# Tail scores of the experts as 64x64 fp32 products of four heads, short tiles scored in one visit, and a new order of the third stage

## The chip, the cores and the metric

The kernel runs on 1 core of one Trainium2 chip. What counts is the device time of one execution, in microseconds (us). "Before" is the median of 3 runs. One execution of it was taken by the profiler, and every row below is of that one.

## What is computed

Three layers follow one another: windowed attention, a gated feed-forward layer with a mixing matrix over the positions, and four experts of causal attention of which each token takes two. The change lies in the third.

```python
# B, S, D, E, Hd = 4, 576, 512, 4, 64
logits = x @ w_gate
topk = np.argpartition(-logits, 2, axis=-1)[..., :2]      # two experts per token, weights w
for e in range(E):
    q = x @ wq[e]
    k = x @ wk[e]
    v = x @ wv[e]
    scores = scale * (q @ k.transpose(0, 2, 1))
    scores = np.where(causal, -1000000000.0, scores)
    scores = scores - scores.max(-1, keepdims=True)
    a = np.exp(scores)
    a /= a.sum(-1, keepdims=True) + 1e-09
    ye = a @ v @ wo[e]
    # out += w * ye where the token chose e
```

## The kernel before

The program has three stages, one behind the other on every engine: attention and the feed-forward layer with their weights (`OPENING`, `FIRST`, `SECOND`), the fold of two weight matrices into `W` (L902, ends near 268 us), and the experts. In the third stage an expert is called a head; two heads make a pair (`pr` is the pair, `o` the head in it), and the two heads of a pair lie in the two halves of the 128 partitions.

A value that must keep fp32 accuracy is held as two f32r tiles, a high part and a low part, and a product is made in three passes (`PASSES`): high by high, high by low, low by high.

Each of the 4 batches has 576 tokens: four tiles of 128 queries (`j` 0 to 3) and a tail of 64 (`j` 4). The columns of q and k are stored with the 64 of the tail first. The third stage consists of these steps, named as in the table `THIRD`:

- `Q` (`project`, L1001): q or k of a pair, half of the columns, one of three passes, 4 products. `qh` and `ql` copy the high part (ScalarE) and subtract for the low part (VectorE).
- `V` and `vr`: values of a tile and the gate's logits; `g` and `h`: the gate.
- `Z` and `sp` (`spread`, L1015): GpSimd zeroes tiles `qt` of 128 columns per pair and copies the tail's q of each head onto its own 64 columns of its own half of the rows. A product with `qt` over all 128 rows then gives both heads of a pair at once, with zeros in the other quarters.
- `S` (`scores_b`): the scores of a tile, one pair of heads per visit. For `j` < 4 it makes products of 64 rows (L1083), two heads at a time. For the tail it makes products of 128 rows with `qt` (L1088): three stretches of 256, 256 and 64 keys by three passes, nine per visit. Scores stand in PSUM tiles `psB`, of which there are two; the two pairs of tile 0 or 1 share one.
- `l`, `e`, `f`, `m`: least value with the mask (VectorE, L1104, L1108), exponential (ScalarE), factors, scaling (GpSimd, L298). `T`, `w`, `R`: transposition in blocks, by way of DRAM. For the last tiles of batch 3 the transposition is made by TensorE (`t`, `c`).
- `A` (`attend_b`, L1192, fp32): attention; `oh`, `ol` copy it as high and low part into `o` tiles, of which there are `OBUFS`.
- `O`, `oc`, `o` (`out_tile`, L1210): the last projection, copy and store.
- `L`, `GH`, `GL`, `BH`, `BL`: the input of a batch is loaded, and its high and low parts are made. The tiles `x` (batches 0 and 2) and `x2` (batches 1 and 3) are used again, so the parts of batch 3 come after batch 1 has been projected. From batch 2 on, GpSimd makes the low part (L263).

`THIRD` lists the steps in one row, and this row is the order in which each engine gets its instructions: nothing is scheduled afterwards. An engine takes its instructions strictly in that order and waits where an input is not there.

The first stage has products of the form that the change brings, at L525 to L533, 64 rows by 64 columns, fp32, heads in the four quarters of the array. A product of fp32 operands stands in the trace as two records.

Of the kernel before, what the change touches and what calls it, by code (L numbers as in the profile page):

```python
# [119 lines left out]
class Dense:  # L120
# [68 lines left out]
    ql0.1.1.0 Q0.0.0.1.0 g0.0.1 g0.0.0 Q0.0.1.1.0 g0.0.5 g0.0.2 g0.0.6 Q0.0.0.1.1 g0.0.3 g0.0.7 Q0.0.1.1.1 g0.0.4 Q1.1.1.1.0 g0.0.8 Q0.0.0.1.2 g0.0.9
    Q0.0.1.1.2 g0.0.10 qh0.0.0.1 Q1.0.0.1.2 g0.0.11 qh0.0.1.1 ql0.0.0.1 GH2.0 Q1.1.1.1.1 g0.0.12 ql0.0.1.1 Q1.1.1.1.2 qh1.0.0.1 g0.0.13 GL2.0 S0.0.0  # L190
    ql1.0.0.1 qh1.1.1.1 L2.2 S0.1.0 GH2.1 l0.0.0 S0.0.1 l0.0.1 l0.1.0 S0.1.1 e0.0.0 l0.0.2 GL2.1 e0.0.1 V1.4.0 l0.0.3 l0.1.1 e0.0.2 V1.4.1 l0.1.2
    e0.0.3 l0.1.3 Q1.1.0.0.0 e0.1.0 ql1.1.1.1 S0.2.0 e0.1.1 f0.0 e0.1.2 Q1.1.0.0.1 l0.2.0 m0.0.0 e0.1.3 l0.2.1 V1.4.2 m0.0.1 e0.2.0 m0.0.2 Q1.1.1.0.0
# [1133 lines left out]
```

## Time and profile before

| | |
|---|---|
| median of 3 runs | 435.45 us (435.08 to 436.15) |
| the profiled execution | 435.67 us |
| its span, first to last instruction | 433.6 us |
| TensorE's granted clock, mean | 0.999 |
| the third stage | from 268 us to the end |
| last product ends | 429.65 us |

The span of the profile is 2.1 us shorter than the time of the same execution. A view by stretches gives the busy time of each engine in each part of the span. The chain of waits goes back from the last instruction to what released it, and lists the pieces in order of time. A group of equal instructions has a mean length, and matrix products overlap with each other: how much of the line a product takes is read from start to next start, not from its length.

### The profile page before, as it was taken

How to read it: one execution, taken by the hardware profiler on the slowest of the kernel's cores; microseconds unless marked ns; L12 is line 12 of the kernel's file. 1: busy time of each engine (PE TensorE's matmuls, PEld its weight loads, DVE VectorE, ACT ScalarE, POOL GpSimd, SP SyncE). 2: the span in 40 equal slices, each digit the busy share in tenths (PEclk: the TensorE clock that was granted, in tenths of full speed). 3: DMA queues.
4: the chain of work that ended last, by engine and by line, in shares of the span. 5: the costliest groups of instructions: out<-in, count | busy, mean ns of one | idle time of the engine just before them, and what ended most of it. 6: DMA issues, size and time to landing. Idle time of an engine off the chain costs nothing.

```text
span 433.6 us, 11406 instructions
## 1 busy us (share of the span) xinstructions
PE 419.6 (97%) x4055; PEld 376.8 (87%) x4055; DVE 306.9 (71%) x1062; ACT 240.3 (55%) x746; POOL 152.8 (35%) x281
## 2 busy tenths in 40 slices
...
GB/s 246 359 337 255 134 219 181 103 325 237 214 258 117 217 165 114 110 83 55 114 256 255 163 104 0 110 2 69 179 237 281 144 204 220 235 227 250 245 232 122
DMA packets 76940, 80.01 MB, mean 185 GB/s; under 512 B 18002, under 2 KB 52946, under 8 KB 76500
## 3 DMA queue, kind: packets, MB, share of 16 engines
...
q8 instruction: 32, 0.52, 0.5%
q14 instruction: 24, 0.20, 0.2%
...
## 4 chain that ended last, share of the span: by engine, by line
PE 82%; DVE 10%; DMA 3%; ACT 3%; issue 1%; SPq 1%; DVEq 0%; ACTq 0%
PE pq L1001 12%; PE pg L750 11%; PE pu L735 11%; PE pv L672 8%; PE pvB L1025 6%; PE pxB L1192 6%; PE pout_None L1210 6%; PE px L646 5%; PE psB L1083 4%; PE pw L902 4%; DVE p L285 2%; PE psB L1088 2%; PE pg L753 2%; DMA carry<-p 2%; PE ps L529 1%
## 5 line engine op out<-in xcount | busy, mean ns | idle before, releaser
L286 ACT ACTIVATE p<-p,st 128x128 f32<-128x128 f32 x144 | 56.4, 393 | 15.8 <-DVE st L285 11.4
L750 PE MATMUL pg<-wsp,vn 128*128 128x288 f32 x384 | 60.3, 297 | 1.3 <-ACT vn L707 1.0
L750 PEld LDWEIGHTS pg<-wsp,vn 128*128 128x128 f32 x384 | 54.2, 188 | 3.8 <-ACT vn L707 1.2
L735 PE MATMUL pu<-x,win 128*128 128x288 f32 x384 | 57.5, 296 | 0.0
L1001 PE MATMUL pq<-x,W 128*128 128x288 f32 x384 | 57.1, 297 | 0.0
L672 PE MATMUL pv<-win,x 128*128 128x512 f32 x216 | 56.1, 398 | 0.0
L735 PEld LDWEIGHTS pu<-x,win 128*128 128x128 f32 x384 | 53.4, 188 | 1.8 <-issue 0.9
L1001 PEld LDWEIGHTS pq<-x,W 128*128 128x128 f32 x384 | 52.5, 188 | 1.7 <-issue 0.8
L1113 ACT ACTIVATE pB<-pB,stB 128x128 f32<-128x128 f32 (+4 forms) x72 | 41.8, 583 | 13.2 <-DVE stB L1104 4.8
L565 POOL TENSOR_TENSOR p<-p,st 128x512 f32<-128x512 f32 (+1 forms) x28 | 29.9, 1071 | 52.4 <-DVE st L563 16.1
L298 POOL TENSOR_SCALAR pB<-pB,stB 128x384 f32<-128x384 f32 (+4 forms) x64 | 35.7, 576 | 28.9 <-ACT pTB L1182 6.8
L672 PEld LDWEIGHTS pv<-win,x 128*128 128x128 f32 x216 | 38.7, 188 | 8.0 <-issue 1.1
L1104 DVE CUSTOM_DVE_ANT_0 pB<-psB,trit 128x128 f32<-128x128 f32 (+3 forms) x64 | 28.4, 485 | 8.5 <-PE psB L1083 8.4
L285 DVE CUSTOM_DVE_ANT_0 p<-ps,relm 128x128 f32<-128x128 f32 x128 | 30.2, 284 | 1.9 <-DMA carry<-p 1.7
L600 POOL TENSOR_SCALAR_AFFINE_SELECT pU<-pT 128x512 f32<-128x512 f32 (+1 forms) x26 | 16.0, 625 | 40.7 <-DMA pT<-carry 27.8
L1139 DVE STREAM_TRANSPOSE pB<-pB 128x1024 f32<-128x1024 f32 (+3 forms) x28 | 26.7, 977 | 1.6 <-POOL pB L298 1.6
L758 DVE TENSOR_TENSOR g<-u,pg 128x288 f32<-128x288 f32 x32 | 14.3, 448 | 18.5 <-PE pg L753 18.3
L1025 PE MATMUL pvB<-W,x 128*128 128x260 f32 x192 | 27.4, 284 | 0.0
L286 ACT ACTIVATION_READ_ACCUMULATOR p<-p,st 128x1 f32 x144 | 27.2, 189 | 0.0
L1192 PE MATMUL pxB<-pTB,vt 128*64 128x128 f32 (+2 forms) x480 | 26.7, 261 | 0.0
L1192 PEld LDWEIGHTS pxB<-pTB,vt 128*64 128x64 f32 (+1 forms) x480 | 23.2, 136 | 3.7 <-issue 1.3
L1210 PE MATMUL pout_None<-wo,o 128*128 128x512 f32 x102 | 26.4, 400 | 0.0
...
## 6 DMA issues: line engine op xcount, KB each, us to landing
...
```

The costliest lines, as they stand in the source:

```text
L285: lambda: nc.vector.tensor_tensor_reduce(s_view, ps_view, tab, -0.125, FLT_MAX, ALU.add, ALU.min, nm),
L286: lambda: nc.scalar.activation(s_view, s_view, AF.Exp, bias=nm, scale=-1.0, accum_out=sm),
L298: nc.gpsimd.tensor_scalar(p, p, r, 0.0, op0=ALU.mult, op1=ALU.add)
L565: ops["m"] = lambda: nc.gpsimd.tensor_tensor(blocks, blocks, sm.unsqueeze(1).unsqueeze(3).to_broadcast([P, 4, n, 32]), op=ALU.mult)
L672: nc.tensor.matmul(pv, x[i][:, k, t0 : t0 + P], win[j][:, k, 512:1024], start=(n == 0 and k == 0), stop=(n == 2 and k == 3))
L735: nc.tensor.matmul(pu[:, :HALF], win[i][:, k, m * P : (m + 1) * P], x[j][:, k, c], start=(n == 0 and k == 0), stop=(n == 2 and k == 3))
L750: nc.tensor.matmul(pg[:, :HALF], vn[i][k][:, m * P : (m + 1) * P], wsp[j][:, k, c], start=(n == 0 and k == 0), stop=False)
L1001: nc.tensor.matmul(pq[:, :HALF], W[i][c0 // CUT][:, k, c0 % CUT : c0 % CUT + P], G[j][:, k, c], start=(n == k == 0), stop=(n == 2 and k == 3))
L1025: nc.tensor.matmul(pv[:, :260], rows, W[j][1][:, k, 512 - CUT :], start=(n == k == 0), stop=(n == 2 and k == 3))
L1113: nc.scalar.activation(part(i), part(i), AF.Exp, bias=st[:, i : i + 1], scale=-1.0, accum_out=st[:, 4 + i : 5 + i])
L1192: nc.tensor.matmul(px[64 * o : 64 * o + 64, pr, :qn], vt[:kb, c, (2 * pr + o) * 64 : (2 * pr + o) * 64 + 64], rhs(pr, c, o), start=(c == 0 ...
L1210: nc.tensor.matmul(po[:, : c.stop - c.start], o2[i][:, pr, :], wos[j][:, pr, c], start=(n == pr == 0), stop=(n == 2 and pr == 1))
```

## The change

The tail's q and k are no longer spread. `whole` (steps `qf`, `kf`) adds high and low part on GpSimd into fp32 tiles: `q4` (64 columns, both pairs at once) and `k4` (576 columns, one pair at a time, one buffer). `scores_b` for the tail then makes 64x64 fp32 products: the head in the pair decides the half of the rows, the pair decides the half of the output's partitions. So the tail's scores now have the pair on the partitions and the head of the pair in the place where the pair was, and `tail_gate`, `row_min` and `read_back` follow. A visit at index 0 takes 256 keys, at index 1 the other 256 and 64, each for all four heads. For tiles 0 and 1 one visit scores both pairs. `OBUFS` goes from 10 to 8, and `THIRD` is another order. `OPENING`, `FIRST`, `SECOND` and the fold are as they were.

```diff
@@ -33,7 +33,7 @@
 FLT_MAX = 3.0e38
 TOK = [(t * 128, min(128, S - t * 128)) for t in range(5)]
 COL = [64, 192, 320, 448, 0]
-OBUFS = 10
+OBUFS = 8
 CARRIED = 6
 PASSES = ((0, 0), (0, 1), (1, 0))
 ORDER = ((0, 1, 2, 3, 4), (4, 0, 1, 2, 3))
@@ -182,52 +182,51 @@
 THIRD = """
-    L1.0 L1.1 L1.2 L1.3 Q0.1.0.1.0 VZ0 VZ1 Z0 Q0.0.0.0.0 Z1 Q0.0.0.0.1 Q0.1.0.1.1 Q0.1.0.1.2 Q0.0.0.0.2 V0.2.0 qh0.1.0.1 qh0.0.0.0 V0.0.0 ql0.1.0.1
...
+    L1.0 L1.1 L1.2 L1.3 Q0.1.0.1.0 VZ0 VZ1 Q0.1.0.1.1 Q0.1.0.1.2 V0.0.0 V0.0.1 Q0.0.0.0.0 V0.0.2 qh0.1.0.1 BH1 Q0.0.0.0.1 ql0.1.0.1 vr0.0 Q0.0.1.0.0
...
 """
@@ -984,9 +983,6 @@
         tag = "qk"[role]
         return get((tag, b), lambda: [wk.tile([P, 2, S], F32R, tag=f"{tag}{i}", name=f"{tag}{b}_{i}") for i in range(2)])
 
-    def tail_heads(b):
-        return get(("qt", b), lambda: [wk.tile([P, 2, P], F32R, tag=f"qt{i}", name=f"qt{b}_{i}") for i in range(2)])
-
     def values(b):
         return get(("vt", b), lambda: wk.tile([P, 5, 260], F32, tag="vt", name=f"vt{b}"))
 
@@ -1008,11 +1004,15 @@
         else:
             lo_part(lo, pq[:, :HALF], hi)
 
-    def spread(b, pr, i):
-        from_, to = heads(b, 0)[i].bitcast(F32), tail_heads(b)[i]
-        for o in range(2):
-            r = slice(64 * o, 64 * o + 64)
-            nc.gpsimd.tensor_scalar(to[r, pr, r], from_[r, pr, 0:64], 1.0, 0.0, op0=ALU.mult, op1=ALU.add)
+    def whole(b, role, pr=None):
+        hi, lo = heads(b, role)
+        if role:
+            to = get(("k4", b), lambda: wk.tile([P, 2, S], F32, tag="k4", name=f"k4_{b}", bufs=1))
+            to, hi, lo = (t[:, pr, :] for t in (to, hi, lo))
+        else:
+            to = get(("q4", b), lambda: wk.tile([P, 2, 64], F32, tag="q4", name=f"q4_{b}"))
+            hi, lo = (t[:, :, 0:64] for t in (hi, lo))
+        nc.gpsimd.tensor_add(to, hi.bitcast(F32), lo.bitcast(F32))
 
     def value(b, t, n):
         pv = bank("pvB", b, t)
@@ -1061,8 +1061,8 @@
 
     def tail_gate(b):
         gt, gq = gate_of(b)
-        for o in range(2):
-            nc.scalar.copy(gq[64 * o : 64 * o + 64, :], gt[0:64, 4, :].rearrange("p (r o) -> p o r", o=2)[:, o, :])
+        for pr in range(2):
+            nc.scalar.copy(gq[64 * pr : 64 * pr + 64, :], gt[0:64, 4, 2 * pr : 2 * pr + 2])
 
     def keys_seen(j):
         return min(S, TOK[j][0] + P)
@@ -1072,20 +1072,23 @@
         two = get(("psB", *key), lambda: psS.tile([P, 2, 512], F32, tag="S", name="psB%d_%d_%d" % key))
         return two[:, :, 256 * pr : 256 * pr + keys_seen(j)] if j < 2 else two
 
-    def scores_b(b, j, pr):
+    def scores_b(b, j, at):
         q0, kn = TOK[j][0], keys_seen(j)
         Q, K = heads(b, 0), heads(b, 1)
-        view = score_bank(b, j, pr)
-        if j < 4:
+        if j == 4:
+            view = score_bank(b, j, at)
+            for c, k0, w in ((0, 64, 256),) if at == 0 else ((0, 320, 256), (256, 0, 64)):
+                for pr in range(2):
+                    for o in range(2):
+                        r = slice(64 * o, 64 * o + 64)
+                        nc.tensor.matmul(view[64 * pr : 64 * pr + 64, o, c : c + w], made["q4", b][r, pr, :], made["k4", b][r, pr, k0 : k0 + w], start=True, stop=True)
+            return
+        for pr in (0, 1) if j < 2 else (at,):
+            view = score_bank(b, j, pr)
             for n, (x_, y_) in enumerate(PASSES):
                 for o in range(2):
                     r = slice(64 * o, 64 * o + 64)
                     nc.tensor.matmul(view[:, o, :kn], Q[x_][r, pr, 64 + q0 : 192 + q0], K[y_][r, pr, 64 : 64 + kn], start=(n == 0), stop=(n == 2))
-        else:
-            T = tail_heads(b)
-            for o, c, k0, w in ((0, 0, 64, 256), (1, 0, 320, 256), (1, 256, 0, 64)):
-                for n, (x_, y_) in enumerate(PASSES):
-                    nc.tensor.matmul(view[:, o, c : c + w], T[x_][:, pr, :], K[y_][:, pr, k0 : k0 + w], start=(n == 0), stop=(n == 2))
 
     def weights(b, j):
         n = 4 if j < 4 else 2
@@ -1103,9 +1106,8 @@
             q0, kn = TOK[j][0], keys_seen(j)
             V.tensor_tensor_reduce(part(i), cut(score_bank(b, j, pr)[:, o, :kn]), cut(trit[:, 512 - q0 : 512 - q0 + kn]), -0.125, FLT_MAX, ALU.add, ALU.min, st[:, i : i + 1])
             return
-        two = score_bank(b, j, i)
-        for o, (c0, w) in enumerate(((0, 256), (256, 320))):
-            V.tensor_tensor_reduce(part(i)[:, c0 // 32 : (c0 + w) // 32], cut(two[:, o, :w]), cut(tritail[:, c0 : c0 + w]), -0.125, FLT_MAX, ALU.add, ALU.min, st[:, 8 + 2 * i + o : 9 + 2 * i + o])
+        for n, (c0, w) in enumerate(((0, 256), (256, 320))):
+            V.tensor_tensor_reduce(part(i)[:, c0 // 32 : (c0 + w) // 32], cut(score_bank(b, j, n)[:, i, :w]), cut(tritail[:, c0 : c0 + w]), -0.125, FLT_MAX, ALU.add, ALU.min, st[:, 8 + 2 * i + n : 9 + 2 * i + n])
         V.tensor_tensor(st[:, i : i + 1], st[:, 8 + 2 * i : 9 + 2 * i], st[:, 9 + 2 * i : 10 + 2 * i], op=ALU.min)
 
     def row_exp(b, j, i):
@@ -1155,7 +1157,7 @@
             src = mid[4 * c0 : 4 * c0 + rows // 32 * m].rearrange("(c k) i a w -> (k i) c (a w)", c=m)
             nc.sync.dma_start(pT[:rows, c0 * 4 * w : (c0 + m) * 4 * w].rearrange("i (c w) -> i c w", c=m), src)
         full = pT[:, : (n + 3) // 4 * 4 * w].rearrange("p (c a e q) -> p c a e q", a=4, e=e, q=32)
-        ready[b, j] = lambda pr, c, o: full[:, c, :, 2 * pr + o, :] if j < 4 else full[: 64 if c == 4 else 128, c, 2 * o : 2 * o + 2, pr, :]
+        ready[b, j] = lambda pr, c, o: full[:, c, :, 2 * pr + o, :] if j < 4 else full[: 64 if c == 4 else 128, c, 2 * pr : 2 * pr + 2, o, :]
 
     homes = ["k0", "k1", "q0", "q1"]
 
@@ -1233,11 +1235,10 @@
         key = [int(k) for k in rest_.split(".")]
         if kind in ("L", "GH", "GL", "BH", "BL"):
             load_g(name)
-        elif kind == "Z":
-            for t in tail_heads(*key):
-                nc.gpsimd.memset(t.bitcast(F32), 0.0)
         elif kind == "VZ":
             nc.gpsimd.memset(values(*key)[64:128, 4, 256:260], 0.0)
+        elif kind in ("qf", "kf"):
+            whole(key[0], "qk".index(kind[0]), *key[1:])
         elif kind in ("qh", "ql"):
             project_take(*key, "hl".index(kind[1]))
         elif kind in ("oh", "ol"):
@@ -1247,7 +1248,7 @@
         elif kind == "O":
             out_tile(*key[:2], key[-1], *key[2:-1])
         else:
-            {"Q": project, "sp": spread, "V": value, "vr": value_take, "h": tail_gate, "S": scores_b, "l": row_min, "e": row_exp, "f": factors, "m": scale, "T": turn_blocks,
+            {"Q": project, "V": value, "vr": value_take, "h": tail_gate, "S": scores_b, "l": row_min, "e": row_exp, "f": factors, "m": scale, "T": turn_blocks,
              "w": send, "R": read_back, "t": turn_b, "c": turn_take, "A": attend_b, "oc": out_take, "o": out_store}[kind](*key)
 
     written = ExitStack()
```

Three places of the order. A row is an instruction, its line, the tile it writes and those it reads; line numbers shift by a few, L1001 is L997 after the change, L1083 is L1091, L298 is L297, L263 is L262.

TensorE at the first scores of batch 0 (`psB0_0` is tile 0, `psB0_1` tile 1), before:

```order
L1083 MATMUL psB0_0_0_4095<-k0_0_3971,q0_0_3872 128x128 x2
L1083 MATMUL psB0_0_0_4095<-k0_1_3972,q0_0_3872 128x128 x2
L1083 MATMUL psB0_0_0_4095<-k0_0_3971,q0_1_3873 128x128 x2
L1083 MATMUL psB0_1_0_4107<-k0_0_3971,q0_0_3872 128x256 x2
L1083 MATMUL psB0_1_0_4107<-k0_1_3972,q0_0_3872 128x256 x2
L1083 MATMUL psB0_1_0_4107<-k0_0_3971,q0_1_3873 128x256 x2
L1083 MATMUL psB0_0_0_4095<-k0_0_3971,q0_0_3872 128x128 x2
L1083 MATMUL psB0_0_0_4095<-k0_1_3972,q0_0_3872 128x128 x2
L1083 MATMUL psB0_0_0_4095<-k0_0_3971,q0_1_3873 128x128 x2
L1083 MATMUL psB0_1_0_4107<-k0_0_3971,q0_0_3872 128x256 x2
L1083 MATMUL psB0_1_0_4107<-k0_1_3972,q0_0_3872 128x256 x2
L1083 MATMUL psB0_1_0_4107<-k0_0_3971,q0_1_3873 128x256 x2
```

and after:

```order
L997 MATMUL pq0_0_0_1_4007<-x0_104,W0_384_3382 128x288 x4
L1091 MATMUL psB0_0_0_4015<-k0_0_3933,q0_0_3864 128x128 x2
L1091 MATMUL psB0_0_0_4015<-k0_1_3934,q0_0_3864 128x128 x2
L1091 MATMUL psB0_0_0_4015<-k0_0_3933,q0_1_3865 128x128 x2
L1091 MATMUL psB0_0_0_4015<-k0_0_3933,q0_0_3864 128x128 x2
L1091 MATMUL psB0_0_0_4015<-k0_1_3934,q0_0_3864 128x128 x2
L1091 MATMUL psB0_0_0_4015<-k0_0_3933,q0_1_3865 128x128 x2
L997 MATMUL pq0_0_0_1_4007<-x1_105,W0_384_3382 128x288 x4
L997 MATMUL pq0_0_1_1_4041<-x0_104,W0_384_3382 128x288 x4
L997 MATMUL pq0_0_1_1_4041<-x1_105,W0_384_3382 128x288 x4
L997 MATMUL pq0_0_0_1_4007<-x0_104,W1_384_3384 128x288 x4
L997 MATMUL pq0_0_1_1_4041<-x0_104,W1_384_3384 128x288 x4
```

The four alternating visits to tiles 0 and 1 became one visit to both pairs of tile 0, and tile 1 stands elsewhere.

TensorE at the first tail scores (`psB0_4`, batch 0, tile 4), before:

```order
L1001 MATMUL pq1_1_1_0_4189<-x20_3811,W1_388_3385 128x288 x4
L1025 MATMUL pvB1_3_4293<-W0_388_3383,x20_3811 128x260 x4
L1088 MATMUL psB0_4_0_4301<-k0_0_3971,qt0_0_3838 128x256
L1088 MATMUL psB0_4_0_4301<-k0_1_3972,qt0_0_3838 128x256
L1088 MATMUL psB0_4_0_4301<-k0_0_3971,qt0_1_3839 128x256
L1088 MATMUL psB0_4_0_4301<-k0_0_3971,qt0_0_3838 128x256
L1088 MATMUL psB0_4_0_4301<-k0_1_3972,qt0_0_3838 128x256
L1088 MATMUL psB0_4_0_4301<-k0_0_3971,qt0_1_3839 128x256
L1088 MATMUL psB0_4_0_4301<-k0_0_3971,qt0_0_3838 128x64
L1088 MATMUL psB0_4_0_4301<-k0_1_3972,qt0_0_3838 128x64
L1088 MATMUL psB0_4_0_4301<-k0_0_3971,qt0_1_3839 128x64
L1083 MATMUL psB0_3_1_4316<-k0_0_3971,q0_0_3872 128x512 x2
```

and after:

```order
L997 MATMUL pq1_1_0_1_4302<-x21_3812,W0_384_3382 128x288 x4
L997 MATMUL pq1_1_0_1_4302<-x20_3811,W1_384_3384 128x288 x4
L1025 MATMUL pvB1_0_4365<-W0_388_3383,x20_3811 128x260 x4
L1084 MATMUL psB0_4_1_4374<-k4_0_4037,q4_0_3936 64x256 x4
L1084 MATMUL psB0_4_1_4374<-k4_0_4037,q4_0_3936 64x64 x4
L1084 MATMUL psB0_4_0_4387<-k4_0_4037,q4_0_3936 64x256 x4
L1025 MATMUL pvB1_2_4400<-W0_388_3383,x20_3811 128x260 x4
L997 MATMUL pq1_0_1_1_4330<-x21_3812,W0_384_3382 128x288 x4
L997 MATMUL pq1_0_1_1_4330<-x20_3811,W1_384_3384 128x288 x4
```

Before, the second pair follows 7 rows later as nine more. After, both visits stand together, 4 products a row, and 128-row products are on both sides.

GpSimd around the low halves of batch 3's input (`x21` from `gf3`), before, from the scaling of tile 4 of batch 0 (`pB0_4`) on:

```order
L298 TENSOR_SCALAR pB0_4_4323<-pB0_4_4323,stB0_4_4324 128x18x32 x2
L298 TENSOR_SCALAR pB0_3_4373<-pB0_3_4373,stB0_3_4374 128x16x32 x4
L1048 TENSOR_TENSOR c2_1_0_4516<-c2_1_0_4516,tie_3392 128x80
L1052 TENSOR_TENSOR ex1_0_4518<-vt1_3836,mx1_0_4519 128x20
L1049 TENSOR_TENSOR c1_1_0_4515<-c1_1_0_4515,c2_1_0_4516 128x80
L263 TENSOR_TENSOR x21_3812<-gf3_4419,x20_3811 128x576
L1055 TENSOR_TENSOR ex1_0_4518<-ex1_0_4518,rk1_0_4517 128x20
L1057 TENSOR_SCALAR sm1_0_4520<-sm1_0_4520 128x5
L263 TENSOR_TENSOR x21_3812<-gf3_4419,x20_3811 128x576
L298 TENSOR_SCALAR pB1_0_4495<-pB1_0_4495,stB1_0_4496 128x4x32 x4
```

and after, from the scaling of tile 3 of batch 0 on:

```order
L297 TENSOR_SCALAR pB0_3_4285<-pB0_3_4285,stB0_3_4286 128x16x32 x4
L1015 TENSOR_TENSOR k4_1_4429<-k1_0_4178,k1_1_4179 128x576 x2
L1015 TENSOR_TENSOR q4_1_4466<-q1_0_4255,q1_1_4256 128x128
L297 TENSOR_SCALAR pB0_4_4395<-pB0_4_4395,stB0_4_4396 128x18x32 x2
L1048 TENSOR_TENSOR c2_1_0_4500<-c2_1_0_4500,tie_3392 128x80
L1052 TENSOR_TENSOR ex1_0_4502<-vt1_3836,mx1_0_4503 128x20
L1049 TENSOR_TENSOR c1_1_0_4499<-c1_1_0_4499,c2_1_0_4500 128x80
L262 TENSOR_TENSOR x21_3812<-gf3_4393,x20_3811 128x576
L1055 TENSOR_TENSOR ex1_0_4502<-ex1_0_4502,rk1_0_4501 128x20
L1057 TENSOR_SCALAR sm1_0_4504<-sm1_0_4504 128x5
L297 TENSOR_SCALAR pB1_2_4518<-pB1_2_4518,stB1_2_4519 128x12x32 x4
L262 TENSOR_TENSOR x21_3812<-gf3_4393,x20_3811 128x576
```

The sums `k4_1` and `q4_1` of batch 1 stand ahead of the scaling of tile 4, the gate steps and the low halves; the spreads and memsets are gone.

## Rows read from the trace of the kernel before

**Rows 1.** The page's busy time (us, share of the span) and instructions of each engine.

```profile
PE 419.6 (97%) x4055; PEld 376.8 (87%) x4055; DVE 306.9 (71%) x1062; ACT 240.3 (55%) x746; POOL 152.8 (35%) x281
```

**Rows 2.** Busy time by stretch of the span, third stage: from:to, length, engines, PEclk, DMA.

```profile
268.00:289.70 21.70, 21.70 (x170) 21.63 (x168) 10.00 (x24) 9.62 (x23) 5.16 (x15) 1.00 0.17 56
289.70:293.00 3.30, 2.56 (x29) 1.99 (x28) 2.06 (x12) 2.63 (x10) 2.51 (x2) 1.00 0.01 2
293.00:426.50 133.50, 133.50 (x1271) 119.67 (x1270) 95.20 (x338) 79.16 (x236) 58.20 (x127) 1.00 0.77 209
```

**Rows 3.** The chain of waits in order of time (start, us, what): the last products.

```profile
428.22 1.43 PE pout L1210 x12
```

**Rows 4.** The chain of waits: tail scores (L1088) and their neighbours.

```profile
302.48 0.48 PE pvB L1025 x4
302.96 0.97 PE psB L1088 x9
...
332.28 2.01 PE psB L1088 x18
...
401.10 1.16 PE psB L1088 x9
```

**Rows 5.** TensorE's instructions in order of time, first stage: 64x64 products, what follows.

```profile
44.54 0.56 PE L525 MATMUL ps<-k,q 64*64 64x192 f32 x8
45.02 0.44 PE L646 MATMUL px<-pU,v 128*64 128x128 f32 x4
...
99.93 0.88 PE L525 MATMUL ps<-k,q 64*64 64x192 f32 x16
100.74 0.44 PE L646 MATMUL px<-pU,v 128*64 128x128 f32 x4
```

**Rows 6.** The chain of waits: ordinary scores (L1083) between other products.

```profile
294.34 0.73 PE psB L1083 x6
295.07 0.73 PE pq L1001 x4
...
296.27 1.07 PE pq L1001 x8
...
326.63 1.25 PE psB L1083 x12
...
364.70 0.46 PE pout_None L1210 x2
```

**Rows 7.** The chain at the first and last scores; last row: the waits of TensorE.

```profile
289.86 1.45 PE psB L1083 x18
...
292.04 0.62 PE psB L1083 x6
...
406.48 1.52 PE psB L1083 x24
...
PE psB L1083 <- DVE stB L1104: 0.7, 1, 0.7
```

**Rows 8.** GpSimd's groups by form: count, busy us, mean ns, idle before.

```profile
L263 POOL TENSOR_TENSOR x<-gf,x 128x576 fp32r<-128x576 f32 x8 | 11.4, 1425 | 3.7 <-ACT x L932 2.4 <-DMA mid<-pB 1.1
...
L1015 POOL TENSOR_SCALAR qt<-q 64x64 fp32r<-64x64 f32 x32 | 8.6, 269 | 27.5 <-ACT q L1007 25.9
...
L263 POOL TENSOR_TENSOR both<-gf,both 128x256 fp32r<-128x256 f32 x4 | 3.0, 739 | 26.5 <-ACT both L942 25.9 <-POOL qt L1015 0.5
...
L1238 POOL MEMSET qt<- 128x256 f32 x8 | 2.2, 317 | 1.1 <-PE psB L1088 1.0
```

**Rows 9.** ScalarE and VectorE in order of time: the last writes of W.

```profile
268.25 0.48 ACT L906 CAST W<-pw 128x388 fp32r<-128x388 f32 x1 [1.63 <-PE pw L902]
...
268.77 0.56 DVE L263 TENSOR_TENSOR W<-pw,W 128x388 fp32r<-128x388 f32 x1 [1.55 <-ACT W L906]
```

**Rows 10.** GpSimd in order of time; then the chain: batch 3's low half, its reader.

```profile
339.78 1.42 POOL L263 TENSOR_TENSOR x<-gf,x 128x576 fp32r<-128x576 f32 x1
...
345.34 0.53 PE pq L1001 x4
```

More of the change, by code (lines that the diff above doesn't have):

```diff
@@ L189 @@
[L189 to L192, printed above, removed]
@@ new lines @@
+    V0.2.2 qh0.1.1.0 Q0.1.1.1.0 vr0.2 ql0.1.1.0 Q0.1.1.1.1 L2.1 g0.0.1 g0.0.0 Q0.1.1.1.2 g0.0.5 g0.0.2 g0.0.6 Q0.0.0.1.0 qh0.1.1.1 g0.0.3 g0.0.7
+    S0.0.0 ql0.1.1.1 g0.0.4 Q0.0.0.1.1 l0.0.0 kf0.1 l0.0.1 l0.0.2 Q0.0.1.1.0 e0.0.0 l0.0.3 g0.0.8 e0.0.1 Q0.0.1.1.1 e0.0.2 g0.0.9 Q0.0.0.1.2 e0.0.3
+    g0.0.10 Q0.0.1.1.2 qh0.0.0.1 g0.0.11 S0.2.1 qh0.0.1.1 ql0.0.0.1 GH2.0 g0.0.12 ql0.0.1.1 V1.4.0 l0.2.2 V1.4.1 L2.2 GH2.1 GL2.0 l0.2.3 V1.4.2 e0.2.2
+    g0.0.13 Q1.1.1.1.0 f0.0 vr1.4 kf0.0 S0.2.0 e0.2.3 S0.1.0 g0.4.1 l0.2.0 l0.2.1 Q1.1.1.1.1 GL2.1 e0.2.0 l0.1.0 Q1.0.1.0.0 l0.1.1 e0.2.1 l0.1.2
@@ new lines @@
+    Q1.1.1.1.2 l0.1.3 e0.1.0 m0.0.0 Q1.0.0.1.0 f0.2 m0.0.1 qh1.1.1.1 Q1.0.0.1.1 m0.0.2 e0.1.1 g0.4.0 ql1.1.1.1 m0.0.3 Q1.0.1.0.1 e0.1.2 g0.4.5 m0.2.0
+    T0.0.0 S0.3.0 e0.1.3 L2.3 m0.2.1 GH2.2 S0.3.1 m0.2.2 w0.0 f0.1 m0.2.3 Q1.0.1.0.2 GL2.2 V1.3.0 T0.2.0 qh1.0.1.0 V1.3.1 Q1.0.0.1.2 ql1.0.1.0 g0.4.2
+    T0.2.1 Q1.1.1.0.0 g0.4.6 qh1.0.0.1 g0.4.3 Q1.1.1.0.1 g0.4.7 m0.1.0 ql1.0.0.1 Q1.1.1.0.2 w0.2 m0.1.1 g0.4.4 Q1.0.0.0.0 g0.4.8 m0.1.2 qh1.1.1.0
+    l0.3.0 V1.3.2 g0.4.9 ql1.1.1.0 m0.1.3 Q1.0.0.0.1 vr1.3 l0.3.1 GH2.3 Q1.1.0.1.0 R0.0 l0.3.2 Q1.1.0.0.0 e0.3.0 GL2.3 l0.3.3 Q1.0.0.0.2 e0.3.1
@@ new lines @@
+    g1.0.3 e1.2.0 GL3.0 l1.2.2 Q2.1.0.1.0 g1.0.7 l1.2.3 Q2.1.0.1.1 e1.2.1 T0.4.0 Q2.1.1.0.1 e1.2.2 Q2.0.1.1.2 T0.4.1 e1.2.3 Q2.1.0.1.2 qh2.0.1.1
+    g1.0.4 Q2.1.1.0.2 w0.4 g1.0.8 qh2.1.0.1 ql2.0.1.1 Q2.1.0.0.2 g1.0.9 qh2.1.1.0 ql2.1.0.1 S1.1.0 g1.0.10 qh2.1.0.0 ql2.1.1.0 g1.0.11 ql2.1.0.0
+    S1.3.0 g1.0.12 g1.0.13 A0.0 l1.1.0 h1 A0.2 l1.1.1 R0.3 oh0.0 l1.1.2 e1.1.0 L3.2 ol0.0 e1.1.1 l1.1.3 Q2.0.0.0.0 f1.2 oh0.2 e1.1.2 Q2.0.0.1.0 ol0.2
+    e1.1.3 m1.2.0 Q2.0.0.1.1 GH3.1 m1.2.1 Q2.0.0.0.1 R0.4 l1.3.0 m1.2.2 Q2.1.1.1.0 l1.3.1 Q2.0.1.0.0 e1.3.0 m1.2.3 f1.1 GL3.1 S1.3.1 e1.3.1 T1.2.0
@@ new lines @@
+    S1.0.0 T1.2.1 m1.1.0 Q2.0.0.0.2 m1.1.1 Q2.1.1.1.1 l1.3.2 qh2.0.0.0 m1.1.2 w1.2 Q2.1.1.1.2 ql2.0.0.0 m1.1.3 Q2.0.0.1.2 e1.3.2 l1.3.3 qf2 Q2.0.1.0.1
+    T1.1.0 qh2.0.0.1 Q2.0.1.0.2 qh2.1.1.1 L3.3 GH3.2 A0.3 ql2.0.0.1 qh2.0.1.0 w1.1 GL3.2 e1.3.3 ql2.1.1.1 ql2.0.1.0 f1.3 A0.4 oh0.3 ol0.3 m1.3.0
+    m1.3.1 A0.1 oh0.4 m1.3.2 ol0.4 V2.2.0 oh0.1 VZ2 m1.3.3 V2.2.1 ol0.1 R1.2 l1.0.0 V2.1.0 l1.0.1 l1.0.2 V2.0.0 e1.0.0 l1.0.3 T1.3.0 GH3.3 V2.1.1
+    e1.0.1 S1.4.0 GL3.3 e1.0.2 S1.4.1 T1.3.1 e1.0.3 BH3 V2.0.1 R1.1 kf2.1 V2.2.2 l1.4.0 w1.3 V2.1.2 vr2.2 Q3.1.1.0.0 l1.4.1 vr2.1 kf2.0 e1.4.0
@@ new lines @@
+    R1.4 e2.2.3 l2.3.0 Q3.1.0.0.1 m2.0.0 Q3.1.1.1.2 l2.3.1 m2.0.1 e2.3.0 m2.0.2 Q3.0.1.0.2 f2.2 m2.0.3 O0.0.2 qh3.1.1.1 T2.0.0 qh3.0.1.0 Q3.1.0.0.2
+    m2.2.0 oc0.0 ql3.1.1.1 m2.2.1 S2.3.1 qh3.1.0.0 w2.0 ql3.0.1.0 e2.3.1 m2.2.2 ql3.1.0.0 S2.1.0 l2.3.2 m2.2.3 A1.3 l2.3.3 qf3 e2.3.2 o0.0 T2.2.0
+    e2.3.3 T2.2.1 A1.0 oh1.3 V3.2.0 oh1.0 ol1.3 V3.1.0 w2.2 ol1.0 V3.1.1 f2.3 V3.4.0 m2.3.0 V3.2.1 V3.2.2 m2.3.1 R2.0 l2.1.0 V3.1.2 l2.1.1 e2.1.0
+    m2.3.2 l2.1.2 A1.4 l2.1.3 e2.1.1 m2.3.3 e2.1.2 e2.1.3 T2.3.0 S2.4.1 VZ3 oh1.4 vr3.2 S2.4.0 vr3.1 ol1.4 T2.3.1 kf3.1 V3.4.1 V3.4.2 V3.0.0 R2.2
```

65 lines of the change are left out of this document (24 added, 41 removed).

## The prediction

> **What bounds the kernel now.** I read the page's busy line first: TensorE is busy for 97% of the span, VectorE for 71%, ScalarE for 55%, GpSimd for 35% [rows 1]. Then I read the busy time by stretch. The third stage, whose order the change rewrites, runs from 268 us to the end. In it TensorE is busy for 21.70 of 21.70 us, then for 2.56 of 3.30 us, then for 133.50 of 133.50 us [rows 2]. So apart from one gap near 291 us, this stage lasts exactly as long as its matrix products stand in line, and TensorE's granted clock is 1.00 throughout, which is the 2.4 GHz level [rows 2]. The chain of waits, read in order of time, says the same: piece after piece is TensorE. From the last product at 429.65 us (428.22 + 1.43) to the end of the span there are another 4 us of copy and store [rows 3]. A change here pays by what it takes out of TensorE's line, and costs by any place where the new order makes TensorE wait. Faster work on the other three engines pays nothing.
>
> **Part 1, the tail scores.** Before, each of the eight visits (four batches, two pairs of heads) is nine 128-row products: three stretches of keys by three f32r passes. In the chain a visit alone is one piece of 0.97 us; five of the eight read 0.96 or 0.97. Two stand together as 2.01 us, and one reads 1.16 us because it follows attention and carries the switch back to 128-row products [rows 4]. Their sum is 5 x 0.966 + 2.01 + 1.16 = 8.0 us. About 0.2 us of the last is that switch, which stays with attention, so 7.8 us go.
>
> Added are twelve fp32 products of 64x64 per batch, each recorded as two: four heads by keys of 256, 256 and 64 columns, one uninterrupted visit per batch in the new order. The kernel already runs this form in its first stage. Eight records of 192 columns (four products, one in each quarter of the array) take from 44.54 to 45.02 us until the next product starts, 0.48 us. Sixteen take from 99.93 to 100.74 us, 0.81 us. So four products side by side add 0.33 us and a visit has 0.15 us on top. That is 1.7 ns per column of four [rows 5]. Four of 256 columns are then 0.44 us, and four of 64 columns 0.11 us (I take 0.14, since short products have the least to hide their loads behind). A visit is 0.15 + 0.44 + 0.44 + 0.14 = 1.17 us.
>
> Such a visit also changes the shape in which the array is used, which the old one did not. What this costs its neighbours I read from the ordinary scores, which are 64-row products: four 128-row products between two score visits take 0.73 us, while eight undisturbed ones take 1.07 us, 0.53 us per four. The two switches cost the neighbours 0.20 us [rows 6]. That makes 1.37 us per visit and 5.5 us for four (the one between 128-row products and attention a little less). **This part gives 7.8 - 5.5 = -2.3 us.** Bounds: if switches were free, 4 x 1.02 = 4.1 us and -3.7 us; if the 0.35 us of fixed cost were twice that, 6.9 us and -0.9 us.
>
> The Trainium skill (TensorEngine Tiling (Array Packing), Key Properties) says that changing the tiling mode drains TensorE, which speaks against this change. The 0.20 us and 0.15 us above agree with it and are in the sum. By the same skill (FP8 and Floating Point Precision, TensorE Precision Notes) true fp32 is four passes; with four heads in the four quarters that is, as an estimate from that page of the Trainium skill, four passes over 576 columns where before stood three passes for each of two pairs, six. By that ratio alone 7.8 us become 5.2 us and the part would give -2.6 us.
>
> **Part 2, short tiles in one visit, and the order.** Counted in the new TensorE order, the ordinary scores stand in 13 uninterrupted runs, where there were 15. A run has a fixed cost: six products of 384 columns alone take 0.73 us, twelve take 1.25 us, so the second six cost 0.52 us and 0.21 us is fixed; with the neighbours' 0.20 us, leaving and coming back is 0.41 us [rows 6]. One of the two runs saved stood behind attention, whose own switch stays, and I count it as 0.3 us. **-0.7 us.** The number of attention runs is the same.
>
> The gap at 291 us goes too. There tiles 0 and 1 of batch 0 are scored in four visits, and the second visit to tile 0 writes into the PSUM tile that VectorE is still reading for the first pair of heads; TensorE waits 0.7 us for VectorE's L1104 in one place alone. The 24 products take from 289.86 to 292.66 us (292.04 + 0.62), 2.80 us, while the 24 of tiles 1 and 0 of batch 3 (the same shapes) take 1.52 us [rows 7]. In the new order tile 0 is scored in one visit before VectorE starts on it, then comes other work. **-1.3 us**, between 0 (the wait moves to the next score bank) and -1.3.
>
> **Part 3, what rides along.** GpSimd loses 32 spreads (8.6 us) and 8 memsets (2.2 us), and gains eight sums of 128x576, the form of its L263 row at 1425 ns, and four of 128x128, for which the 739 ns of 128x256 is an upper bound [rows 8]: 11.4 + at most 3.0 against 10.8, so 1 to 3.6 us more on an engine that has 100 us free in this stage (58.20 busy of 133.50 in its long stretch [rows 2]). I cost it at nothing. Its cover is distance: in the new order each batch's tail scores stand at least 17 us of TensorE work behind the last product that feeds its q4 and k4. The path between is one copy, one subtraction and two sums of 1.43 us. (For such distances I add the products along the new order: 0.53 us per four of L1001, 0.48 per four of L1025, 0.46 per two of L1210, and the runs as priced here [rows 4, 6].) The sums of k4 have one buffer, so the sums of batch b+1 wait for the tail scores of batch b, and everything behind them in GpSimd's queue waits too: the scaling of tile 4, gate steps, and the low halves of batch 3's input. The smaller OBUFS holds nothing up: the ninth pair of o tiles is wanted by attention of batch 2, tile 0, long after the projection of batch 0, tile 0, has read the first. The new start asks for the second part of W after 12 products, at 268.2 + 1.6 = 269.8 us, high part, and at 270.3 us, low part; they are written by 268.73 and 269.33 us [rows 9]. So it waits for nothing, by 1 us. The end has the same sequence of kinds (transposes, attention of tiles 4 and 0, two projections), so the 4 us behind the last product stay.
>
> **Sum.** -2.3 - 0.7 - 1.3 = -4.3 us on the profiled execution of 435.67 us (span 433.6 us): 431.4 us. That execution lies 0.2 us above the median of 435.45 us, so about 431.2 to 431.4 us; I say 431.3 us.
>
> **Rivals.** About 0.3% (1.3 us) is what can be told from no change.
>
> A, new waits eat part of it. The old stage stands at TensorE's limit, so any order can only add waits. Places where the new one is short: the scores of batch 3, tile 3 come 2.2 us of products behind the last projection they read (in the old order the shortest was 2.0 us), and the PSUM bank for attention of batch 3, tile 3, is wanted 1.4 us after the last product of the projection that held it. Against it: the shortest distance between a score run and the one whose PSUM tile it takes over grew from 1.8 to 2.9 us. Two to four waits the size of the 0.7 us one [rows 7] give 1.4 to 2.8 us: 432.7 to 434.1 us, still faster.
>
> B, waits give back 3 to 5.6 us: 434.2 to 436.8 us, no difference. The same as A with the gap at 291 us merely moved, or with GpSimd falling behind for a while.
>
> C, slower: GpSimd's queue. In the new order the last low half of batch 3's input stands behind a memset that waits for attention of batch 0 to end, behind a scaling, and after the k4 sums of batch 1, which wait for TensorE. From there TensorE has one tail visit, three value groups and one projection group, 1.4 + 3 x 0.48 + 0.53 = 3.4 us, until it reads that half, which takes 1.42 us to make; before, it was made by 341.20 us and read at 345.34 us [rows 10]. From the point where GpSimd comes more than 2 us late, TensorE waits microsecond for microsecond. To end slower than before, it must be over 2 + 4.3 + 1.3 = 7.6 us late; 9 us late gives 431.3 + 7 = 438 us. GpSimd is busy for 44% of the long stretch [rows 2], and the change adds 3.6 us at most; being late by 7.6 us at that one place would need its waits there to pile up, which they do nowhere in the old trace where TensorE would see it.
>
> D, the four products don't run side by side: the 1.02 us of streaming per batch (0.44 + 0.44 + 0.14) become four times that, 3.06 us more in each of four batches, +12.2 us, 443.5 us. The sixteen records in 0.81 us [rows 5] speak against it; the operands lie in the same two halves of the partitions.
>
> **How the numbers follow.** Forecast 0.62; A 0.20; B 0.10; C and others that lose over 5.6 us 0.06; D 0.02. Faster is the forecast and A: 0.82. Same is B: 0.10. Slower: 0.08. The range begins at 430.2 us (switches nearly free in part 1, less 1.1 us) and goes to 434.2 us, the end of A; outside lie B, C and D with 0.18 and a little below.
>
> **What would show it.** In the profile of the changed kernel: four visits of 24 records of 64x64 in the third stage, each about 1.2 us to the next start, and 128-row groups of four beside them at 0.63 to 0.73 us (part 1). No idle TensorE near the first scores (part 2). TensorE busy for all of the stretch from 268 us to its last product, which ends near 425.3 us, with 4 us behind it. Wrong would be: visits over 1.6 us; TensorE idle behind GpSimd's x or k4 rows, or behind VectorE's L1104; an end more than 4.5 us behind the last product.

## The result, and the profile after

| | before | changed |
|---|---|---|
| median | 435.79 us (435.08 to 436.15, 4 runs) | 430.28 us (429.94 to 430.90, 4 runs) |
| ratio | | 0.9877 (95% interval 0.9858 to 0.9896) |
| the profiled execution | 435.67 us, span 433.6 us | 430.43 us, span 428.3 us |

The change gains 5.5 us by the medians against its runs of before, and 5.2 us between the two profiled executions. The forecast was 431.3 us: right in sign, within the range, and 1 us too cautious.

The page's busy line of the changed kernel, to be read beside [rows 1]:

```profile
PE 414.8 (97%) x4079; PEld 371.0 (87%) x4079; DVE 310.7 (73%) x1062; ACT 239.4 (56%) x746; POOL 154.2 (36%) x253
```

TensorE lost 4.8 us of busy time, and its share stayed at 97%: what bounds the kernel is the same. The busy time by stretch (from:to, length, engines, clock), beside [rows 2]:

```profile
268.00:282.00 14.00, 14.00 (x113) 14.00 (x112) 6.91 (x12) 7.48 (x17) 1.20 (x2) 1.00 0.26 85
282.00:290.00 8.00, 8.00 (x67) 7.34 (x67) 5.00 (x25) 4.94 (x18) 4.06 (x8) 1.00 0.01 3
290.00:420.00 130.00, 130.00 (x1302) 115.51 (x1300) 97.49 (x337) 77.87 (x233) 64.23 (x111) 1.00 0.79 214
```

The stretch with 2.56 of 3.30 us is gone, the clock stands at 1.00 (2.4 GHz) as before, and no idle stretch of TensorE is left in the stage. The chain of waits of the changed kernel (start, us, what) shows the first scores, the four tail visits (L1084) with what stands beside them, and the last product, beside [rows 3, 4, 7]:

```profile
283.85 0.82 PE psB L1091 x12
...
306.40 0.47 PE pvB L1025 x4
306.87 1.14 PE psB L1084 x24
308.01 0.67 PE pvB L1025 x4
...
339.77 1.14 PE psB L1084 x24
...
366.81 1.70 PE pxB L1194 x38
...
368.56 0.98 PE psB L1084 x18
...
391.86 1.14 PE psB L1084 x24
393.00 4.08 PE pxB L1194 x72
...
422.64 1.42 PE pout L1212 x12
```

Eight old visits of about 1 us became four of 1.14 us (in batch 2 the rows of attention and scores overlap, so its row is short). The last product ends at 424.06 us instead of 429.65, with 4.2 us behind it instead of 4.0.

GpSimd's new rows by form (count, busy us, mean ns, idle before), beside [rows 8]:

```profile
L1015 POOL TENSOR_TENSOR k<-k,k 128x576 f32<-128x576 f32 x8 | 11.4, 1433 | 2.6 <-DVE k L262 1.1 <-PE psB L1084 0.9 <-DMA gf<-g_dram 0.5
...
L1015 POOL TENSOR_TENSOR q<-q,q 128x128 f32<-128x128 f32 x4 | 1.9, 463 | 6.2 <-DVE q L262 6.2
```

They are 13.3 us in place of 10.8, and the sum of `k4` stood 0.9 us behind a tail visit (L1084), the wait by its one buffer that the prediction named.

Where the time went is read best by adding, over the third stage, the time from the start of each product to the start of the next: 161.31 us before, 155.90 us after. Of the 5.41 us, tail scores are 3.40 (7.98 to 4.58), ordinary scores 1.59 (19.33 to 17.74), attention 0.50. Projections, values and output moved by 0.2 us or less each.

### The profile page after: what moved, and what is told of

Read it like the earlier page. It is cut to its first block, busy times and chain, and to the rows that moved or that the text cites. A ratio compares the mean times of both kernels' runs of the same rounds, so it can differ in the third digit from the quotient of the medians.

```text
span 428.3 us, 11426 instructions
## 1 busy us (share of the span) xinstructions
PE 414.8 (97%) x4079; PEld 371.0 (87%) x4079; DVE 310.7 (73%) x1062; ACT 239.4 (56%) x746; POOL 154.2 (36%) x253
## 4 chain that ended last, share of the span: by engine, by line
PE 85%; DVE 8%; DMA 2%; ACT 2%; issue 1%; SPq 0%; ACTq 0%; DVEq 0%
PE pg L749 12%; PE pq L997 12%; PE pu L734 10%; PE pv L671 9%; PE pvB L1025 6%; PE pxB L1194 6%; PE pout_None L1212 6%; PE px L645 6%; PE psB L1091 4%; PE pw L901 4%; PE pg L752 2%; DVE p L284 2%; PE ps L532 1%; DMA st_wc<-in_wcat 1%; PE ps L528 1%
## 5 line engine op out<-in xcount | busy, mean ns | idle before, releaser
L997 PE MATMUL pq<-x,W 128*128 128x288 f32 x384 | 56.8, 297 | 0.0
L997 PEld LDWEIGHTS pq<-x,W 128*128 128x128 f32 x384 | 52.5, 188 | 1.6 <-issue 0.8
L297 POOL TENSOR_SCALAR pB<-pB,stB 128x384 f32<-128x384 f32 (+4 forms) x64 | 35.7, 575 | 28.9 <-DVE stB L1124 14.3
```

The lines of the kernel that those rows point to most:

```text
L297: nc.gpsimd.tensor_scalar(p, p, r, 0.0, op0=ALU.mult, op1=ALU.add)
L997: nc.tensor.matmul(pq[:, :HALF], W[i][c0 // CUT][:, k, c0 % CUT : c0 % CUT + P], G[j][:, k, c], start=(n == k == 0), stop=(n == 2 and k == 3))
```

## The experiments

The theory was that of the prediction: TensorE's line is the time, and three things shortened it (the tail's form, fewer runs of scores, the gap at 291 us). The first four kernels take the parts apart. "Sum" below is the start-to-start sum of stage 3. The kernels ran in several groups, each beside runs of the kernel before, whose medians lie between 435.14 and 435.79 us; a ratio is taken within a group, and medians of different groups can differ by some 0.6 us for that reason alone. The smaller differences below therefore rest on the sums of the traces.

**The new form in the old order** (`old_order_new_tails`). Only the rows of `THIRD` that the form needs were moved, so that both visits of a tail stand together:

```diff
-... S0.4.0 m0.2.2 R0.0 ... S0.3.1 l0.4.0 ... S0.4.1
+... S0.4.0 S0.4.1 m0.2.2 l0.4.0 l0.4.1 R0.0 ... S0.3.1
-        for pr in (0, 1) if j < 2 else (at,):
+        for pr in (at,):
```

> The form alone: the order of before, with the tail's scores as 64x64 fp32 products (both visits of a tail together, the sums on GpSimd in place of the spreads, OBUFS 8). Short tiles keep one visit per pair. Theory (the form is worth the 7.8 us of old visits less four times 1.14 + 0.20 us): 2.4 us faster than before, 433.3 us, with TensorE's gap at 291 us still there. Rival 'the order is everything': no difference, 435.7 us. Rival 'the form is everything': 5.2 us faster, 430.5 us.

Measured: 434.21 us (ratio 0.9969, 0.9957 to 0.9981), sum 160.05. TensorE's instructions in order of time at the first tail (start, us, what; in brackets the idle time before), then the waits of TensorE in the stage (us, times, longest):

```profile
302.07 0.64 PE L1025 MATMUL pvB<-W,x 128*128 128x260 f32 x4
302.64 1.21 PE L1084 MATMUL psB<-k,q 64*64 64x256 f32 x24
305.22 0.98 PE L1091 MATMUL psB<-k,q 64*128 64x512 f32 x6 [1.38 <-DVE stB L1110]
...
PE psB L1091 <- DVE stB L1110: 1.4, 1, 1.4
PE psB L1091 <- DVE stB L1107: 0.7, 1, 0.7
PE ptB L1173 <- DVE stB L1110: 0.2, 1, 0.2
```

The visit is as short as in the changed kernel, but both PSUM tiles for scores are now filled in one go, and the next scores, `S0.3.1`, wait 1.38 us until VectorE's L1110 has read the first of them through for both halves; a further 0.24 us went at a transposition. The 0.7 us is the old wait of [rows 7]. Without the two new waits the form is worth 1.26 + 1.62 = 2.9 us here. So the new form asks for an order in which the next score visit stands further away.

**One visit for tiles 0 and 1 in the old kernel** (`old_order_one_visit`): the kernel before, its table alone edited for tiles 0 and 1 of each batch.

```diff
-... S0.0.0 ql1.0.0.1 qh1.1.1.1 L2.2 S0.1.0 GH2.1 l0.0.0 S0.0.1 l0.0.1 l0.1.0 S0.1.1 ...
+... S0.0.0 S0.0.1 ql1.0.0.1 qh1.1.1.1 L2.2 S0.1.0 S0.1.1 GH2.1 l0.0.0 l0.0.1 l0.1.0 ...
```

> Short tiles in one visit alone: the order of before and the old zero-padded tails; for tiles 0 and 1 the second pair's products are moved up behind the first pair's. Theory (the gap at 291 us comes from the second pair writing into a PSUM tile that VectorE reads): the 24 products there take 1.5 us instead of 2.8, 1.3 us faster than before, 434.4 us. Rival 'the wait only moves to the next score tile': no difference, 435.7 us, with as much idle TensorE a few us later.

Measured: 434.26 us (ratio 0.9975, 0.9962 to 0.9988). No wait of TensorE is left in the stage, and the 24 products of the first scores take 1.58 us where they took 2.79: 1.2 us. The wait was removed and not moved.

**The new order with the old tail scores** (`new_order_old_tails`): the changed kernel with `spread`, `qt` and the nine f32r products put back at the same places of the new order.

```diff
-                        nc.tensor.matmul(view[64 * pr : 64 * pr + 64, o, c : c + w], made["q4", b][r, pr, :], ...
+                    nc.tensor.matmul(view[:, o, c : c + w], T[x_][:, pr, :], K[y_][:, pr, k0 : k0 + w], start=(n == 0), stop=(n == 2))
```

> The form alone undone: the new order and one visit for short tiles, OBUFS 8, but the tail's scores as zero-padded f32r products of 128 rows, with spreads and memsets where the sums stood. Theory: four visits of about 1.34 us with their switches become eight of 0.97 us, 2.4 us slower than the changed kernel, 432.8 us. Rival 'the order is everything': 430.4 us, as the changed kernel. Rival 'the form is everything': 435.7 us, as before.

Measured: 433.93 us (ratio 0.9956, 0.9940 to 0.9972), sum 159.38. Its chain at the four tails (nine products of each pair, both pairs together):

```profile
307.70 2.02 PE psB L1088 x18
...
341.37 2.01 PE psB L1088 x18
...
370.89 2.21 PE psB L1088 x18
...
395.29 2.02 PE psB L1088 x18
```

161.31 - 159.38 = 1.9 us are the order's, and 159.38 - 155.90 = 3.5 us are the form's, 1.1 us more than was expected of it. The next two kernels ask why.

**Each visit of a tail by itself** (`tails_apart`): the changed kernel with the two visits of each tail parted by other products, such as

```diff
-... f0.3 V1.0.0 qh1.1.0.1 BL2 h0 S0.4.1 ql1.1.0.0 ql1.1.0.1 R0.2 S0.4.0 ...
+... f0.3 S0.4.1 V1.0.0 qh1.1.0.1 BL2 h0 ql1.1.0.0 ql1.1.0.1 R0.2 S0.4.0 ...
```

> The changed kernel with the two visits of each tail set apart by one group of four 128-row products (in batch 2 the last behind it, with the k4 sums of batch 3 after it). Theory (a visit has 0.15 us of its own and 0.20 us at its neighbours that is the switch of shape): four more switches, 1.4 us slower, 431.8 us, the eight visits summing to 5.2 us from start to next start instead of 4.6. Rival 'a switch hides behind the loads of weights': 430.4 us.

Measured: 431.47 us (ratio 0.9911, 0.9892 to 0.9929), 1.2 us more by the medians. The chain at the first tail, where L1083 is the tail's line:

```profile
305.51 0.71 PE psB L1083 x16
306.21 0.68 PE pvB L1024 x4
306.89 0.59 PE psB L1083 x8
307.48 0.67 PE pvB L1024 x4
```

0.71 + 0.59 instead of 1.14 is 0.16 us for the visit, and the neighbours pay the rest: the four parted tails cost 0.33 to 0.37 us more each, 1.4 us in all (sum 157.31). That is the 0.15 + 0.20 us of the prediction. So the price of an additional excursion was right, and the mis-sizing lies elsewhere.

**Two visits at other neighbours** (`visits_between_long`): batch 2's moved behind `V3.4.1`, batch 3's ahead of `O1.3.2`.

```diff
-... A1.4 ... T2.3.0 S2.4.1 VZ3 oh1.4 vr3.2 S2.4.0 ... kf3.1 V3.4.1 V3.4.2 ...
+... A1.4 ... T2.3.0 VZ3 oh1.4 vr3.2 ... V3.4.1 S2.4.1 S2.4.0 kf3.1 V3.4.2 ...
-... O1.3.2 o2.0 oc1.0 S3.4.0 o0.1 T3.3.1 e3.2.1 S3.4.1 o1.0 A2.3 ...
+... S3.4.0 S3.4.1 O1.3.2 o2.0 oc1.0 o0.1 T3.3.1 e3.2.1 o1.0 A2.3 ...
```

> The changed kernel, only the places of two tail visits altered: batch 2's stands between two long products of V3.4 instead of right behind the last 64-row products of a tail's attention, batch 3's between two output products instead of right before an attention. Theory (a visit costs its 1.14 us plus 0.20 at its neighbours where these are 128-row products, and next to nothing beside where a neighbour has changed its shape already): the visits stay at 1.14 and the sum of stage 3 rises from 155.9 by 0.3 to 0.4, time 430.6. Rival (the neighbours' cost is the same anywhere, and the 3.5 us that the form was worth in the new order come from elsewhere): sum 155.9 and 430.3.

Measured: 431.06 us (ratio 0.9907, 0.9892 to 0.9923), sum 156.42. Its chain at batch 2:

```profile
367.29 1.75 PE pxB L1193 x40
369.05 0.67 PE pvB L1024 x4
369.72 1.14 PE psB L1083 x24
370.86 1.15 PE pvB L1024 x8
```

The visits still take 1.14 us; the place behind attention was worth 0.34 us, the one ahead of attention 0.21 us. So the chosen places do save: the last products of a tail's attention have 64 rows already, and an attention makes its own change of shape whatever stands ahead of it (4.08 us behind the visit and behind the output product alike).

**The sums on GpSimd three times, then twice** (`sums_thrice`, `sums_twice`). Rival C said that GpSimd's queue could become what TensorE waits for; here the sums are repeated with the same result.

```diff
-        nc.gpsimd.tensor_add(to, hi.bitcast(F32), lo.bitcast(F32))
+        for _ in range(3):
+            nc.gpsimd.tensor_add(to, hi.bitcast(F32), lo.bitcast(F32))
```

> The changed kernel with the sums of high and low half that the tail scores read (line 1015, 8 of 1433 ns and 4 of 463 ns) made three times each, so 26.6 us more on GpSimd, 6.6 us more ahead of each batch's tail scores. Theory (the sums are far enough ahead of the scores that read them): no idle TensorE in stage 3, 430.3 within 0.8. Rival (the queue of GpSimd is what the tail visits nearly wait for): TensorE stands before the visits of one or more batches, 1 to 6 us each, 432 to 440.

Measured: 441.26 us (ratio 1.0140, 1.0126 to 1.0153), slower than before. My theory of ample distance fell. But the tail visits don't wait, as the rival had it; everything else does. First GpSimd in the changed kernel, in order of time:

```profile
311.68 1.44 POOL L1015 TENSOR_TENSOR k<-k,k 128x576 f32<-128x576 f32 x1 [0.46 <-DMA gf<-g_dram]
313.07 0.47 POOL L1015 TENSOR_TENSOR q<-q,q 128x128 f32<-128x128 f32 x1
314.43 1.63 POOL L297 TENSOR_SCALAR pB<-pB,stB 128x576 f32<-128x576 f32 x2 [0.89 <-DVE stB L1124]
```

and with the sums made three times, GpSimd and then TensorE:

```profile
311.19 8.96 POOL L1016 TENSOR_TENSOR k<-k,k 128x576 f32<-128x576 f32 x6
320.10 1.53 POOL L1016 TENSOR_TENSOR q<-q,q 128x128 f32<-128x128 f32 x3
321.61 1.48 POOL L297 TENSOR_SCALAR pB<-pB,stB 128x576 f32<-128x576 f32 x2
323.05 0.36 POOL L1049 TENSOR_TENSOR c<-c,tie 128x80 f32<-128x80 f32 x1
...
326.47 2.85 PE L1195 MATMUL pxB<-pTB,vt 128*64 128x128 f32 x32 [2.79 <-DVE k L262]
```

The scaling of tile 4 starts 7.2 us later; behind it stand the gate's small steps, and ScalarE and VectorE wait for those in their own fixed order. The chain goes from the sums through the scaling and two gate steps on GpSimd to six exponentials and a copy on ScalarE, one subtraction on VectorE, and to attention, which waits 2.79 us. By the sum the stage is 11.6 us longer. Ten idle stretches of TensorE, this one the longest, hold 7.2 us of it. Another 1.6 us is the clock. The busy time by stretch, as in the table of the changed kernel above:

```profile
322.50:327.40 4.90, 2.11 (x33) 1.63 (x31) 3.59 (x9) 3.19 (x11) 3.26 (x7) 1.00 0.40 79
327.40:330.80 3.40, 3.40 (x26) 3.07 (x23) 3.23 (x17) 2.84 (x12) 0.46 (x1) 0.50 1.00 197
```

Behind the wait of 2.79 us the granted clock stood at 0.50 (1.2 GHz) for 3.4 us, and pairs of attention's products took 0.21 us from start to start there instead of 0.11. For the remaining 2.8 us the products start later without the trace showing TensorE idle. Is any part of this paid with the sums made once? They were made twice:

```diff
-        for _ in range(3):
+        for _ in range(2):
```

> The changed kernel with the sums that the tail scores read made twice each, 13.3 us more on GpSimd (3.3 us a batch), after three times each gave 441.3 and waits of TensorE behind GpSimd's later work (the scaling of weights and small sums queued behind them). Theory (GpSimd has a slack of some us at each place, and only what goes over it is paid: with 6.6 us a batch more, the first wait of length was 2.8 us at 326.5): no wait over 0.5 us at the first three places, 430.3 to 431.5. Rival (GpSimd's queue has no slack in this order, so each us of it costs 0.4 us of the end as 26.6 us cost 10.9): 435 to 436.

Measured: 430.94 us (ratio 0.9894, 0.9879 to 0.9908); sum 156.99. The first 13.3 us more cost 0.7 us by the medians (1.1 by the sum, all of it near 354 us), the second 13.3 us cost 10.3 us, 1.6 us of them by the clock. So there is slack, as an estimate 2 to 4 us at the two places of the longest waits: 6.6 us more cost 2.8 us near 326 us, and 2.9 us more (two sums of `k4`) cost 1.0 us near 354 us. The sums made once cost TensorE nothing, but the slack is not ample.

**A shorter attention for tails** (`last_keys_adjacent`, `last_keys_outside`). The tails' attention leaves to 64 rows and comes back once for each pair of heads. Two orders of its products, the first:

```diff
+            cs = (4, 0, 1, 2, 3) if j == 4 and pr else tuple(range(j + 1))
-            for c in range(j + 1):
+            for c in cs:
-... start=(c == 0), stop=(c == j))
+... start=(c == cs[0]), stop=(c == cs[-1]))
```

> The changed kernel, in the attention of a tail the second pair of heads begins with the key tile of 64 rows instead of ending with it, so that the four products of 64 rows stand together: one excursion to 64 rows and back fewer in each of three tails (batch 1's tail visit stands behind the attention and had shared it). An excursion is read at 419.10 us of the changed kernel as 0.29 us (152, 100, 149, 100 ns to the next start instead of 52 each). Theory: attention 0.9 less, 25.5 to 24.6, time 429.4. Rival (the products wait for that last tile's weights, or the switch is paid elsewhere): attention unchanged and 430.3 or more.

Measured: 429.38 us (429.26 to 430.23; ratio 0.9870, 0.9857 to 0.9882), the lowest median of all, though its runs overlap those of the changed kernel, whose ratio was 0.9877: by the ratios the two can't be told apart, and the gain is read from the traces. Chain at the last tail, changed kernel:

```profile
418.71 2.34 PE pxB L1194 x48
```

and with the four short products together:

```profile
418.06 2.05 PE pxB L1195 x48
```

The 0.29 us are saved there and at batch 0, 0.15 us at batch 2, whose run had ended with the short products right before output products, and nothing at batch 1. Together that is 0.70 us by the sum (155.20), of the 0.9 expected. With the short products first and last instead:

```diff
-            cs = (4, 0, 1, 2, 3) if j == 4 and pr else tuple(range(j + 1))
+            cs = (4, 0, 1, 2, 3) if j == 4 and not pr else tuple(range(j + 1))
```

> As the run before, but the first pair begins with the tile of 64 rows and the second ends with it: the two excursions merge with the change of shape that the start and the end of the attention make anyway. Theory: as many changes fewer as with the products together, and one more where batch 1's attention is followed by batch 2's tail visit: attention 0.9 to 1.1 less, 429.2 to 429.4. Rival (entering 64 rows from full products costs as much more as it saves): 429.8 to 430.3.

Measured: 429.97 us (ratio 0.9881, 0.9867 to 0.9895). By the sum (155.61) only 0.29 us are saved, 0.15 at batches 1 and 3; this theory fell. At batch 0 other attentions stand on both sides, and at batch 2 one stands ahead, so the short products that now come first make a change of shape of their own. At batches 1 and 3 the attention stands behind 128-row products, and the short products at its start still paid half of an excursion's 0.29 us, as the rival had it in part.

## Why the prediction was right, and where its sizes were off

**The bound** held. Nothing in the new order makes TensorE wait, so the sum of start-to-start times is the stage.

**Part 1, the tail scores: -2.3 us, and -3.5 us measured** in the new order (2.9 in the old one, without the waits it made there). The visit was right: 1.17 predicted, 1.14 measured. Two sizes were off. What goes was taken as 7.8 us from the places of the old order; at the new places the old form takes 2.01 + 2.01 + 2.12 + 2.11 = 8.26 us start to start, since the switch behind attention, which I left with attention, and the one ahead of attention in batch 3 belong to the visits as well, 0.1 us each. The other half is between the two pairs, which now always stand together: the second pair's first product, behind the first pair's 64-column products, takes 200 to 203 ns to the next start where the others of its form take about 120. And the 0.20 us per visit for neighbours, 0.8 us in all, was counted as wholly new. Measured against the old form at the same places, the four values ahead of the first visit grew from 476 to 564 ns, but the four behind it only from 565 to 583: the old visit had made its follower pay too, though it used all 128 rows. Batch 2's visit stands beside products of 64 rows and gave back 0.18 us. Together the neighbours cost 0.17 us. 4.58 + 0.17 = 4.75 us against 8.26 is the 3.5 us. The place where the price was read, an excursion inserted into undisturbed products, was the wrong comparison; the parted visits paid just that price.

The Trainium skill (TensorEngine Tiling (Array Packing), Key Properties) says that a change of tiling mode drains TensorE. The trace agrees that a change costs and gives the size (that a drain is its cause no run shows): 0.29 us for an excursion of two products within attention and 0.35 us for parting a visit. By the four passes of the Trainium skill (FP8 and Floating Point Precision, TensorE Precision Notes) the new form would, as an estimate from that page, take 4/6 of the old one; the trace gives 4.75 of 8.26 us, 0.58, and decides.

**Part 2: -2.0 us, and 1.9 us measured** by the new order with the old form. Of these the gap gave 1.2 us (1.3 predicted), shown by the old kernel with one visit alone. That leaves 0.7 us for the fewer runs, the predicted size, but as a remainder: no kernel shows it by itself. Of it 0.44 us lie in the ordinary scores (18.16 us in the old order with one visit, 17.72 us in the new order with the old form), as two runs fewer at the fixed 0.21 us would have it; the rest is spread over other products, attention above all.

**Part 3: nothing, and nothing measured** with the sums as they are. The reason given, distance, covers only the tail visits themselves. What counts is the queue behind the sums, and there the margin is 2 to 4 us by the estimate above.

**The rivals.** A and B, new waits, didn't come in this order; they did where the form was put into the old one, 1.6 us of them, at PSUM tiles. The prediction had counted that distance for the new order alone (grown from 1.8 to 2.9 us), and there it held. C is a true mechanism at another price: it needs twice the sums' time again, and its place is the gate and the scaling, not batch 3's low half. D fell with 1.14 us a visit. The range's lower end, 430.2 us, held the result by only 0.1 us, because it allowed 1.1 us for the whole of part 1.
